# One core, attention and two MLPs: the first table load goes ahead of ScalarE's transfers, the fillers read another tile, and the norm's work moves to the end of the first MLP's steps

## The chip, the core and the metric

The kernel runs on one core of one Trainium2 chip. The time is device microseconds (us) of one launch. The engines are named as in the profile: PE (TensorE, matmuls; PEld is its weight load), ACT (ScalarE), DVE (VectorE), POOL (GpSimd), SP (SyncE, which here only issues transfers). An entry such as ACTq or SPq is an instruction of that engine's queue that the engine itself does not execute, here the issue of a transfer.

## What is computed

Three stages follow each other on 1536 tokens (2 sequences of 768) of width 512, all in float32.

```python
scores = scale * np.matmul(q, k.transpose(0, 1, 3, 2))      # 8 heads of 64
scores = np.where(keep, scores + bias, -1e9)                # keep: first 8 keys, or 96 back
x = softmax(scores) @ v                                     # -> 1536 x 512
h = x @ w_in                                                # 512 -> 2048
x = (h * np.tanh(softplus(h))) @ w_out                      # Mish, 2048 -> 512
xn = x / np.sqrt(np.mean(x * x, -1) + 1e-6) * rms_g
out = (silu(xn @ w_gate) * (xn @ w_val)) @ w_out2           # 512 -> 1536 -> 512
```

The weights arrive as 64-bit words. The kernel turns each piece of them, on the chip, into a high and a low part in a 32-bit format that PE multiplies; a product is then three matmuls (high by high, high by low, low by high).

## The kernel before, in words

**Attention.** There are 48 units: 2 sequences, 4 pairs of heads, 6 tiles of 128 queries. A tile looks at 128 or 256 keys. `scores` (L635) multiplies on PE into two of four PSUM banks, so a unit's scores wait until `soft` has read those of two units before. Behind each unit's scores stands one small matmul as a filler (L649), and in the first four rounds `WARM` larger ones as well (L271, called at L768); the fillers' results are read by nobody. `soft` (L654) adds the bias on DVE (L662) and takes exp on ACT (L672); `norm` (L683) divides on POOL; `transp`, `evac` and `pv` do the product with v. `make_bias` (L620) halves the bias of one head into that of the next on DVE. The bias tile itself is started by four ACT instructions (L743) from maps that DVE makes (L319 to L328). The eight first weight pieces are converted during attention by a fixed plan; the first step of a piece is an ACT instruction on the loaded words (L152).

**The order.** Nothing is scheduled for the author: each engine runs its instructions in the order in which the code emits them. At the start SP and ACT both issue the transfers for the first pair of heads: SP q and k (L245 to L247), ACT v, in two halves of four transfers each (`tiles_v`, L224). ACT's first table load and its first activation (L259) stand behind all eight. The fillers at the very start (L274) read a tile of ones that DVE writes (L261); the fillers in attention read the bias tile (`fill`, L618).

A transfer's completion is counted on one of eight counters that are used in turn, so an issue can wait for the landing of the transfer that last used its counter.

**The first MLP** has 32 steps. A step takes two of the 16 hidden chunks for one block of 384 tokens (four blocks): `products` puts 24 matmuls (L360) in two banks; `mish1` (L495) turns them into g by a chain of tanh, a table load, arctan, sin (ACT, L380 to L386), a multiplication (DVE, L389), a high part (ACT, L486) and a low part (DVE, L490); 18 matmuls (L412) of the step before, in `flush`, stand on PE between this step's products and the next step's. `begin` puts the five bit operations of a next weight piece on DVE (2.7 us for a piece) at the end of the step, two pieces in every eighth step. Steps 24 to 31 hold the last chunks: after step 25's 18 matmuls block 0 is complete, after step 27's block 1, and so on.

**The norm** (`rms_norm`, L451) of a complete block is a list of deferred pieces: squares with row sums on ACT (L457), a power on POOL (L461, L464), the scaling on DVE (L468), and four transposing splits (`split_y`, L436: three PE transposes into bank `s3` at L440, a high part on ACT at L444, a low part on DVE at L445). The squares write their unused result into the same bank `s3`.

```python
        for i in range(2):
            mish.tanh(i)
        do_deferred()
        flush(0)
        do_deferred()
        mish.cosine()
```

`do_deferred` takes one piece from the list. In the first MLP it is called on both sides of `flush`, ahead of the chain's table load. **The second MLP** (`mlp2`, L538, 48 steps of 24 products and 9 accumulating matmuls) calls it in the same two places, and takes what is left of the list.

Of the kernel before, what the change touches and what calls it, by code (L numbers as in the profile page):

```python
# [10 lines left out]
BF16 = mybir.dt.bfloat16  # L11
# [6 lines left out]
P = 128  # L18
# [4 lines left out]
NK = DM // P  # L23
# [3 lines left out]
TB = BT // P  # L27
NBLK = B * S // BT
WPIECE = 512
BANK = 512  # L30
# [8 lines left out]
SLOTS = (10, 14)  # L39

NW_EARLY = 8
WARM = 2

AHEAD = {-4: (0, 2), -3: (2, 4), -2: (4, 6), -1: (6, 8), 0: (8, 12), 1: (12, 16)}

# [5 lines left out]
def tile_attention_mish_swiglu(  # L51
# [16 lines left out]
    pe, act, dve, pool, sp = nc.tensor, nc.scalar, nc.vector, nc.gpsimd, nc.sync  # L68
# [18 lines left out]
    def bank(tag, bufs=1):  # L87
        return psum.tile([P, BANK], F32, tag=tag, bufs=bufs, name=nm(tag))

    def mm_bank():  # L90
        return bank("mm", 4)
# [125 lines left out]
    room = [xypool.tile([P, TB * DM], F32, tag="xy", name=nm("x")) for _ in range(NBLK)]  # L217
# [6 lines left out]
    def tiles_v(v_t, b, p, own=slice(0, NT), queue=None):  # L224


        queue = queue or sp
        vp = v[b][:, p * P : (p + 1) * P]
        vr = vp.rearrange("(t r) e -> r t e", r=P)
        queue.dma_start(v_t[:, own, :], vr[:, own, :])  # L230
        n, last = max(own.start - 1, 0), own.stop - 1
        win = slice(NT + n, NT + last)
        for r in (slice(GLOBAL_MAX, 64), slice(64, P)):
            queue.dma_start(v_t[r, win, :], vr[r, n:last, :])
        queue.dma_start(
            v_t[0:GLOBAL_MAX, win, :],
            vp[0:GLOBAL_MAX].rearrange("r (o e) -> r o e", o=1).to_broadcast(
                (GLOBAL_MAX, last - n, P)
            ),
        )  # L240

    for m in range(2):
        tok = slice(m * BT, (m + 1) * BT)
        own, win = slice(m * TB, (m + 1) * TB), slice(NT + (m and 2), NT + 2 + 3 * m)
        sp.dma_start(q_first[:, tok], qT[0, 0][:, tok])  # L245
        sp.dma_start(k_first[:, own, :], kT[0, 0][:, own, :])
        sp.dma_start(k_first[:, win, :], kT[0, 0][:, win, :])  # L247
        tiles_v(v_first, 0, 0, own, act)

    small = cpool.tile([P, 28], F32, tag="small", name="small")  # L250
    half, mhalf = small[:, 0:1], small[:, 1 : 1 + TB]
# [5 lines left out]
    dve.memset(mhalf, -0.5)  # L257
    dve.memset(half_pi, HALF_PI)
    act.activation(primed, half, AF.Exp)  # L259
    first = room[1][:, 10 * P : 12 * P].bitcast(BF16)  # L260
    dve.memset(first, 1.0)  # L261
    dve.memset(least[:, 0:1], 1.0)
    dve.memset(least[:, 1:4], 0.0)
    dve.memset(most, 0.0)
# [4 lines left out]
    def warm(ps, n, x):  # L269
        for _ in range(n):  # L270
            pe.matmul(ps, x[:, 0:P], x, start=True, stop=True)  # L271

    for _ in range(4):
        warm(mm_bank(), 3, first)  # L274
    ident = cpool.tile([P, P], F32, tag="ident", name="ident")
    make_identity(nc, ident)

# [117 lines left out]
    def begin(n):  # L395
        for _ in range(n):
            begun.append(Piece(started[0]))
            begun[-1]("b3")
            started[0] += 1
# [30 lines left out]
    deferred = []  # L430

    def do_deferred():
        if deferred:
            deferred.pop(0)()

    def split_y(y, blk, kc):  # L436
        t = hl.tile([P, 2, BT], F32R, tag="hl", name=nm("hl"))
        tr = bank("s3")
        for m in range(TB):
            pe.transpose(  # L440
                tr[:, m * P : (m + 1) * P], y[:, m, kc * P : (kc + 1) * P], ident
            )
        g = gcol[:, kc : kc + 1]
        act.activation(t[:, 0, :], tr[:, 0:BT], AF.Copy, scale=g)  # L444
        dve.scalar_tensor_tensor(  # L445
            t[:, 1, :], tr[:, 0:BT], g, t[:, 0, :].bitcast(F32),
            op0=ALU.mult, op1=ALU.subtract,
        )
        ys.setdefault(blk, []).append(t)

    def rms_norm(blk):  # L451
        y = sums[blk]
        ss = cpool.tile([P, 2, TB], F32, tag="ss", name=nm("ss"), bufs=2)

        def square(m):
            junk = bank("s3")
            act.activation(junk, y[:, m, :], AF.Square, accum_out=ss[:, 0, m : m + 1])  # L457

        def inverse():
            square(TB - 1)  # L460
            pool.tensor_scalar(  # L461
                ss[:, 1, :], ss[:, 0, :], 1.0 / DM, 1.0e-6, op0=ALU.mult, op1=ALU.add
            )
            pool.tensor_tensor(ss[:, 0, :], ss[:, 1, :], mhalf, op=ALU.pow)  # L464

        def scale():
            for m in range(TB):
                dve.tensor_scalar(  # L468
                    y[:, m, :], y[:, m, :], ss[:, 0, m : m + 1], None, op0=ALU.mult
                )  # L470

        deferred.append(lambda: [square(m) for m in range(TB - 1)])
        deferred.append(inverse)
        deferred.append(scale)
        deferred.extend([lambda kc=kc: split_y(y, blk, kc) for kc in range(NK)])

    pend = []

# [16 lines left out]
    def mish1(s, mish):  # L495

        blk, cs = s // 2 % NBLK, chunks(s)
        for i in range(2):
            mish.tanh(i)
        do_deferred()  # L500
        flush(0)
        do_deferred()
        mish.cosine()
        old = begun[:]
        del begun[:]
        for piece in old[:1]:
            piece("hi")
        for i in range(2):
            mish.times(i)
        for piece in old[:1]:  # L510
            piece("lo")
        gt = [split_hi(mish.t[:, i, :]) for i in range(2)]
        for piece in old[1:]:
            piece("hi")
        for i in range(2):
            split_lo(gt[i], mish.t[:, i, :])
        for piece in old[1:]:
            piece("lo")
        begin(BEGUN1[s])

        def later():
            def done(m):
                if m == TB - 1 and cs[1] == NC1 - 1:
                    rms_norm(blk)

            for c, g in zip(cs, gt):
                accumulate("out", g, c, blk, done)

        pend.append(later)
# [57 lines left out]
    def attention_banded():  # L587
        fresh()
        mm = [mm_bank() for _ in range(4)]
        with ExitStack() as st:  # L590
# [24 lines left out]
            biases = bp.tile([P, H, 3 * P], BF16, tag="bias", name="bias")  # L615
            bias, bias0 = biases[:, :, 0 : 2 * P], biases[:, :, 2 * P :]

            fill = biases.rearrange("p h k -> p (h k)")[:, 0:BANK]  # L618

            def make_bias(h):  # L620

                dve.tensor_scalar(  # L622
# [7 lines left out]
            first = []  # L630
# [4 lines left out]
            def scores(u):  # L635
                b, p, t = u
                n = width(t) // P
                banks = mm[2:4] if units.index(u) % 2 else mm[0:2]
                for j in range(2):
                    r = slice(64 * j, 64 * j + 64)  # L640
                    pe.matmul(  # L641
                        banks[j][:, 0 : n * P],
                        qs[b, p][r, t * P : (t + 1) * P],
                        ks[b, p][r, 0, :] if t == 0 else ks[b, p][r, t : t + NT : NT - 1, :],
                        start=True,
                        stop=True,
                    )

                pe.matmul(  # L649
                    banks[1][:, 3 * P :], fill[:, 0:P], fill[:, 0:P], start=True, stop=True  # L650
                )
                sc[u] = banks

# [105 lines left out]
            for i in range(-4, nu + 2):  # L759

                def tick(slot, i=i):
                    for k, op in plan.get((i, slot), ()):
                        pieces[k](op)

                if i + 4 < nu:
                    scores(units[i + 4])
                if i < 0:
                    warm(bank("s3"), WARM, fill)  # L768
                if 0 <= i < nu:
                    transp(units[i])  # L770
                if i >= 2:
                    pv(units[i - 2])
                for j in range(*AHEAD.get(i - nu, (0, 0))):
                    c, kc = divmod(j, NK)
                    if kc == 0:
                        first.append(mm_bank())
                    products(first[c], "in", c, xs[0], (kc,))
                if i == nu - 2:
                    mish_first = Mish(first)
                if nu - 2 <= i < nu:  # L780
                    mish_first.tanh(i - nu + 2)
                if 1 <= i <= nu:
                    evac(units[i - 1])
                if 0 <= i + 3 < nu:
                    soft(units[i + 3], tick)
                if 0 <= i + 2 < nu:
                    norm(units[i + 2], tick)
                if -3 <= i < 3:
                    make_bias(i + 5)
                if i >= 2:  # L790
                    evac_out(units[i - 2])
                if i % NT == 2 and 0 <= i // NT:
                    for load, n in ((load_qk, 2), (load_v, 1)):
                        if i // NT + n < B * NPAIR:
                            load(*divmod(i // NT + n, NPAIR))
                tick(3)
                if i == nu - 1:
                    for piece in pieces:
                        piece.rest()
                if i == nu:  # L800
                    mish1(0, mish_first)
# [155 lines left out]
```

## Time and profile before

| | |
|---|---|
| median of 3 runs | 695.7 us (694.32 to 696.01) |
| the profiled execution, its own time | 695.73 us |
| its span from first to last instruction | 693.9 us |
| PE, PEld busy | 673.5 us (97%), 585.2 us (84%) |
| DVE, ACT, POOL busy | 450.2 us (65%), 386.1 us (56%), 68.8 us (10%) |
| granted TensorE clock, mean | 0.993 |
| moved by DMA | 54.20 MB, 78 GB/s over the span |

The busy share of PE is that of a pipelined engine whose ends are modelled. The profiled execution is the source of all durations below; 1.8 us of its own time lie outside of its span. A line of the timeline gives the start in us, how long it lasted in us, the engine, the line of the code, the operation, what is written and read, and how many like instructions are merged in it; in brackets stands how long the engine had been idle before it, and what ended that.

### The profile page before, as it was taken

To read this page: it belongs to the slowest core of one execution; us is meant where nothing else is said; L and a number is where in the kernel's file an instruction comes from. 1 tells how busy PE (TensorE), PEld (TensorE's weight loads), DVE (VectorE), ACT (ScalarE), POOL (GpSimd) and SP (SyncE) were. 2 spreads that over 40 slices of the span, in tenths; PEclk is the share of its full clock that TensorE was granted. 3 is DMA by queue.
4 is the path that set the end of the run, shared out by engine and by line. 5 is a ranking of instruction groups with operands and counts; after the bars stand their busy time and mean duration, and the time that the engine had idled before them with its cause. 6 is when DMAs were issued, how large, how long until landed. Compare 5 with 4: busy or idle time off the path is not lost.

```text
span 693.9 us, 10039 instructions
## 1 busy us (share of the span) xinstructions
PE 673.5 (97%) x3764; PEld 585.2 (84%) x3764; DVE 450.2 (65%) x1067; ACT 386.1 (56%) x722; POOL 68.8 (10%) x128
## 2 busy tenths in 40 slices
PE   7999999999999999999889999999999999999997
PEld 2666668999999999999678889999999999999996
DVE  4878764887788778875866788884268774331232
ACT  3989887888888888887788524322122222111111
POOL 1676770000000000000000001000000000000000
PEclk8999999999999999999999999999999999999999
DMA  8767630122123212211111122230022200010111
GB/s 261 233 209 236 176 104 31 62 91 61 63 68 91 84 60 71 82 61 61 64 58 61 32 79 74 74 109 31 1 61 91 77 16 1 0 46 1 46 47 50
DMA packets 26729, 54.20 MB, mean 78 GB/s; under 512 B 2609, under 2 KB 14641, under 8 KB 26673
## 3 DMA queue, kind: packets, MB, share of 16 engines
q1 hardware_dynamic: 25136, 52.77, 23.9%
q10 hardware_dynamic: 1536, 0.72, 0.4%
q8 instruction: 31, 0.51, 0.3%
q14 instruction: 26, 0.20, 0.1%
HBM read 50.34 MB, written 3.15 MB: 77 GB/s over the span
## 4 chain that ended last, share of the span: by engine, by line
PE 80%; DVE 9%; ACT 9%; issue 1%; DMA 1%; SPq 0%; ACTq 0%
PE mm L360 42%; PE s L412 29%; PE mm L641 3%; PE s L726 2%; ACT e L672 2%; PE s L706 2%; ACT L384 1%; DVE bits L175 1%; DVE e L662 1%; DVE bits L169 1%; ACT d L385 1%; ACT d L386 1%; DVE w L194 1%; DVE g L490 1%; DVE d L389 1%
## 5 line engine op out<-in xcount | busy, mean ns | idle before, releaser
L360 PE MATMUL mm<-hl,w 128*128 128x384 f32 x1920 | 349.6, 336 | 0.0
L360 PEld LDWEIGHTS mm<-hl,w 128*128 128x128 f32 x1920 | 336.2, 188 | 6.9 <-issue 1.0
L412 PE MATMUL s<-w,g 128*128 128x512 f32 x1008 | 246.9, 393 | 4.3 <-ACT g L486 3.0
L412 PEld LDWEIGHTS s<-w,g 128*128 128x128 f32 x1008 | 187.0, 188 | 43.5 <-ACT g L486 4.5
L553 ACT ACTIVATE r<-mm 128x384 f32<-128x384 f32 x48 | 23.5, 490 | 135.3 <-PE mm L360 135.2
L554 DVE TENSOR_TENSOR r<-r,mm 128x384 f32<-128x384 f32 x48 | 26.4, 550 | 68.7 <-ACT r L553 68.7
L424 DVE TENSOR_TENSOR x<-x,s 128x512 f32<-128x512 f32 x60 | 40.2, 686 | 40.2 <-PE s L412 40.2
L486 ACT ACTIVATE g<-r 128x384 fp32r<-128x384 f32 x48 | 25.2, 525 | 69.9 <-DVE r L554 69.9
L389 DVE TENSOR_TENSOR d<-d,mm 128x384 f32<-128x384 f32 x64 | 32.5, 550 | 46.1 <-ACT d L386 46.1
L672 ACT ACTIVATE e<-e,s 128x256 f32<-128x256 f32 (+1 forms) x96 | 46.2, 482 | 11.5 <-DVE s L662 11.1
L691 POOL TENSOR_SCALAR e<-e,s 128x256 f32<-128x256 f32 (+1 forms) x96 | 47.8, 513 | 38.9 <-DVE bias L622 15.1
L169 DVE SCALAR_TENSOR_TENSOR bits<-stage,bits 128x512 int32<-128x512 int32 x68 | 48.2, 708 | 2.1
L175 DVE SCALAR_TENSOR_TENSOR bits<-stage,bits 128x512 int32<-128x512 int32 x68 | 47.2, 694 | 2.0
L490 DVE TENSOR_TENSOR g<-r,g 128x384 fp32r<-128x384 f32 x48 | 26.8, 559 | 28.4 <-ACT g L486 28.4
L486 ACT ACTIVATE g<-d 128x384 fp32r<-128x384 f32 x64 | 33.4, 526 | 16.4 <-DVE d L389 14.5
L384 ACT ACT_TABLE_LOAD x32 | 41.1, 1283 | 0.6
L194 DVE TENSOR_TENSOR w<-bits,w 128x512 fp32r<-128x512 f32 x60 | 41.3, 688 | 0.0
L380 ACT ACTIVATE d<-mm 128x384 f32<-128x384 f32 x64 | 30.4, 492 | 17.5 <-PE mm L360 15.8
L380 ACT ACT_TABLE_LOAD x31 | 39.8, 1283 | 0.5
L662 DVE CUSTOM_DVE_ANT_0 e<-mm,bias 128x256 f32<-128x256 f32 (+1 forms) x96 | 35.2, 396 | 5.1 <-PE mm L641 3.2
L190 ACT ACTIVATE w<-bits 128x512 fp32r<-128x512 f32 x60 | 36.9, 616 | 0.0
L641 PE MATMUL mm<-k,q 64*128 64x256 f32 (+1 forms) x168 | 31.9, 410 | 2.6 <-DVE s L662 2.6
(83 smaller groups left out, 509.7 us busy)
## 6 DMA issues: line engine op xcount, KB each, us to landing
stage<-in_w_out_dram SPq DMA_DIRECT2D x28, 512.0 KB, 3.2
stage<-in_w_in_dram SPq DMA_DIRECT2D x16, 512.0 KB, 4.3
stage<-in_w_gate_dram SPq DMA_DIRECT2D x12, 512.0 KB, 3.5
stage<-in_w_val_dram SPq DMA_DIRECT2D x12, 512.0 KB, 3.4
k<-in_kT_dram SPq DMA_DIRECT2D x7, 704.0 KB, 4.1
out_dram<-x SPq DMA_DIRECT2D x12, 256.0 KB, 2.1
q<-in_qT_dram SPq DMA_DIRECT2D x7, 384.0 KB, 4.7
v<-in_v_dram SPq DMA_DIRECT2D x7, 384.0 KB, 6.1
```

The costliest lines, as they stand in the source:

```text
L169: dve.scalar_tensor_tensor(self.bits, self.lw, 29, self.bits, op0=ALU.logical_shift_right, op1=ALU.bitwise_or,)
L175: dve.scalar_tensor_tensor(self.bits, self.hw, -1073741824, self.bits, op0=ALU.bitwise_and, op1=ALU.bitwise_or,)
L194: engine.tensor_tensor(self.wt[:, 1, :], self.fl, self.wt[:, 0, :].bitcast(F32), op=ALU.subtract)
L360: pe.matmul(ps[:, 0:BT], w[:, wi, col], xs[kc][:, xi, :], start=kc == 0 and i == 0, stop=kc == NK - 1 and i == 2,)
L380: act.activation(self.t[:, i, :], self.h[i], AF.Tanh, scale=0.5)
L384: act.preload_act_table_set("trig_and_small")
L412: pe.matmul(acc[m], gt[:, gi, tok], w[:, wi, :], start=c % 4 == 0 and i == 0, stop=c % 4 == 3 and i == 2,)
L486: act.activation(gt[:, 0, :], x, AF.Copy)
L641: pe.matmul(banks[j][:, 0 : n * P], qs[b, p][r, t * P : (t + 1) * P], ks[b, p][r, 0, :] if t == 0 else ks[b, p][r, t : t + NT : NT - 1, :] ...
L662: dve.tensor_tensor_reduce(e[:, j, 0:n], banks[j][:, 0:n], bias0[:, h, :] if t == 0 else bias[:, h, :], scale=-0.125, scalar=3.0e38, op0=A ...
L672: act.activation(e[:, j, 0:n], e[:, j, 0:n], AF.Exp, scale=-1.0, bias=s[:, 0, j : j + 1], accum_out=s[:, 1, j : j + 1],)
L691: pool.tensor_scalar(e[:, j, 0:n], e[:, j, 0:n], s[:, 3, j : j + 1], 0.0, op0=ALU.mult, op1=ALU.add,)
```

## The change

Three things are changed. At the start, ACT's first activation, and with it the table load, comes ahead of ACT's transfers; of those only the first half of v stays on ACT, and the second half is issued by SP behind q and k. The fillers in attention read the tile of ones instead of the bias tile, and the first four rounds have one large filler instead of two. In the norm, all three squares and the power are one piece, the scaling and the first split are one piece, and the first MLP takes one piece a step, at the end of the step just ahead of `begin`, instead of two pieces around `flush`. The second MLP still takes two.

```diff
-WARM = 2
+WARM = 1
@@ the transfers for the first pair of heads
         sp.dma_start(q_first[:, tok], qT[0, 0][:, tok])
         sp.dma_start(k_first[:, own, :], kT[0, 0][:, own, :])
         sp.dma_start(k_first[:, win, :], kT[0, 0][:, win, :])
-        tiles_v(v_first, 0, 0, own, act)
+        if m:
+            tiles_v(v_first, 0, 0, own)
@@
     act.activation(primed, half, AF.Exp)
-    first = room[1][:, 10 * P : 12 * P].bitcast(BF16)
-    dve.memset(first, 1.0)
+    tiles_v(v_first, 0, 0, slice(0, TB), act)
+    ones = room[1][:, 10 * P : 12 * P].bitcast(BF16)
+    dve.memset(ones, 1.0)
@@ rms_norm
         def inverse():
-            square(TB - 1)
+            for m in range(TB):
+                square(m)
             pool.tensor_scalar(
                 ss[:, 1, :], ss[:, 0, :], 1.0 / DM, 1.0e-6, op0=ALU.mult, op1=ALU.add
             )
@@
-        deferred.append(lambda: [square(m) for m in range(TB - 1)])
         deferred.append(inverse)
-        deferred.append(scale)
-        deferred.extend([lambda kc=kc: split_y(y, blk, kc) for kc in range(NK)])
+        deferred.append(lambda: [scale(), split_y(y, blk, 0)])
+        deferred.extend([lambda kc=kc: split_y(y, blk, kc) for kc in range(1, NK)])
@@ mish1
         for i in range(2):
             mish.tanh(i)
-        do_deferred()
         flush(0)
-        do_deferred()
         mish.cosine()
@@
         for piece in old[1:]:
             piece("lo")
+        do_deferred()
         begin(BEGUN1[s])
@@ attention_banded
-            fill = biases.rearrange("p h k -> p (h k)")[:, 0:BANK]
-
@@ scores
-                    banks[1][:, 3 * P :], fill[:, 0:P], fill[:, 0:P], start=True, stop=True
+                    banks[1][:, 3 * P :], ones[:, 0:P], ones[:, 0:P], start=True, stop=True
@@ the rounds
                 if i < 0:
-                    warm(bank("s3"), WARM, fill)
+                    warm(bank("s3"), WARM, ones)
```

How the order moves is seen in three places. Lines of the changed code are up to two higher or one lower than those of before.

ACT at the start of the program, before (`x` is the room that holds v, `small` the tile of constants):

```order
L230 DMA x_84<-in_v_dram 128x3x128
L234 DMA x_84<-in_v_dram 32x2x128
L234 DMA x_84<-in_v_dram 64x2x128
L235 DMA x_84<-in_v_dram 32x2x128
L230 DMA x_84<-in_v_dram 128x3x128
L234 DMA x_84<-in_v_dram 32x3x128
L234 DMA x_84<-in_v_dram 64x3x128
L235 DMA x_84<-in_v_dram 32x3x128
L259 ACT_TABLE_LOAD
L259 ACTIVATE small<-small 128x1
L299 TENSOR_LOAD flag_i
L743 ACTIVATE bias<-x_85 128x128 x2
```

and now:

```order
L260 ACT_TABLE_LOAD
L260 ACTIVATE small<-small 128x1
L230 DMA x_84<-in_v_dram 128x3x128
L234 DMA x_84<-in_v_dram 32x2x128
L234 DMA x_84<-in_v_dram 64x2x128
L235 DMA x_84<-in_v_dram 32x2x128
L301 TENSOR_LOAD flag_i
L742 ACTIVATE bias<-x_85 128x128 x2
```

The load and the first activation went from behind eight issues to ahead of four; the other four stand on SP between its last L247 and its own load of the flag.

DVE in step 27 of the first MLP, before (`x_84` is block 0's sum, `d` and `g` are this step's):

```order
L175 SCALAR_TENSOR_TENSOR bits_3507<-stage_3292,bits_3507 128x512
L468 TENSOR_SCALAR x_84<-x_84,ss_3488 128x512 x3
L389 TENSOR_TENSOR d_3541<-d_3541,mm_3515 128x384
L389 TENSOR_TENSOR d_3541<-d_3541,mm_3516 128x384
L194 TENSOR_TENSOR w_3575<-bits_3507,w_3575 128x512
L490 TENSOR_TENSOR g_3580<-d_3541,g_3580 128x384
L490 TENSOR_TENSOR g_3582<-d_3541,g_3582 128x384
L154 TENSOR_SCALAR bits_3586<-stage_3364 128x512
```

and now:

```order
L175 SCALAR_TENSOR_TENSOR bits_3507<-stage_3288,bits_3507 128x512
L391 TENSOR_TENSOR d_3541<-d_3541,mm_3515 128x384
L391 TENSOR_TENSOR d_3541<-d_3541,mm_3516 128x384
L194 TENSOR_TENSOR w_3568<-bits_3507,w_3568 128x512
L492 TENSOR_TENSOR g_3573<-d_3541,g_3573 128x384
L492 TENSOR_TENSOR g_3575<-d_3541,g_3575 128x384
L471 TENSOR_SCALAR x_84<-x_84,ss_3484 128x512 x3
L447 SCALAR_TENSOR_TENSOR hl_3582<-s_567_3583,small,hl_3582 128x384
L154 TENSOR_SCALAR bits_3589<-stage_3360 128x512
```

The scaling of block 0 went from ahead of the step's multiplications to behind its low parts, and the first split's low part stands right behind it.

PE between steps 27 and 28, before (`mm_3602` and `mm_3603` are step 28's products, `s_560` to `s_562` the accumulators):

```order
L412 MATMUL s_562_3550<-w_3056,g_3503 128x512 x3
L360 MATMUL mm_3602<-hl_182,w_2688 128x384 x3
...
L360 MATMUL mm_3603<-hl_185,w_2904 128x384 x3
L440 MATMUL s_574_3632<-ident,x_84 128x128 x3
L412 MATMUL s_560_3548<-w_3065,g_3580 128x512 x3
```

and now:

```order
L414 MATMUL s_562_3546<-w_3052,g_3495 128x512 x3
L442 MATMUL s_567_3583<-ident,x_84 128x128 x3
L362 MATMUL mm_3605<-hl_182,w_2684 128x384 x3
...
L362 MATMUL mm_3606<-hl_185,w_2900 128x384 x3
L414 MATMUL s_560_3544<-w_3061,g_3573 128x512 x3
```

The first split's transposes of block 0 stand ahead of step 28's products now, where they stood behind them.

## Rows read from the trace of the kernel before

**Rows 1.** The page, part 1: busy time, share of the span, instructions.

```profile
PE 673.5 (97%) x3764; PEld 585.2 (84%) x3764; DVE 450.2 (65%) x1067; ACT 386.1 (56%) x722; POOL 68.8 (10%) x128
```

**Rows 2.** Timeline of the first 21 us.

```profile
7.38 0.29 DVE L325 TENSOR_TENSOR x<-x 128x128 f32<-128x128 f32 x1
...
7.73 1.28 ACT L259 ACT_TABLE_LOAD   x1 [7.73 <-DMA x<-in_v_dram]
...
9.13 1.10 ACT L743 ACTIVATE bias<-x 128x128 bf16<-128x128 f32 x4
...
9.98 0.29 PE L649 MATMUL mm<-bias 128*128 128x128 bf16 x1 [3.27 <-ACT bias L743]
...
10.33 0.80 SPq L119 DMA_DIRECT2D stage<-in_w_in_dram  x2
...
11.23 1.22 PE L641 MATMUL mm<-x,x 64*128 64x256 f32 x4
...
12.49 0.42 DVE L662 CUSTOM_DVE_ANT_0 e<-mm,bias 128x256 f32<-128x256 f32 x1 [1.59 <-PE mm L641]
...
13.46 1.23 PE L641 MATMUL mm<-x,x 64*128 64x256 f32 x4
13.46 0.24 DVE L622 TENSOR_SCALAR bias<-bias 128x384 bf16<-128x384 bf16 x1
...
19.84 0.50 ACT L672 ACTIVATE e<-e,s 128x256 f32<-128x256 f32 x1
...
20.34 0.66 ACT L152 ACTIVATE bits<-stage 128x512 f32<-128x512 f32 x1
```

**Rows 3.** Waits of SP's queue, 0 to 40 us: total, times, longest.

```profile
SPq L119 <- DMA x<-in_v_dram: 0.7, 1, 0.7
```

**Rows 4.** Issues at 5.3 and 10.3 us: KB each, us to landing.

```profile
x<-in_kT_dram SPq DMA_DIRECT2D x2, 192.0 KB, 4.6
stage<-in_w_in_dram SPq DMA_DIRECT2D x1, 512.0 KB, 5.4
```

**Rows 5.** Half microseconds: busy PE, PEld, DVE, ACT, POOL, granted clock, DMA share, GB/s.

```profile
9.00:9.50 0.50, 0.00 (x0) 0.00 (x0) 0.00 (x0) 0.49 (x4) 0.00 (x0) 0.53 0.39 92
...
15.50:16.00 0.50, 0.50 (x3) 0.32 (x4) 0.39 (x3) 0.50 (x3) 0.06 (x1) 0.64 1.13 424
```

**Rows 6.** Timeline, first MLP: step 26 begins at 317.59, step 25's end.

```profile
317.59 4.35 PE L360 MATMUL mm<-hl,w 128*128 128x384 f32 x24
...
318.95 1.02 DVE L490 TENSOR_TENSOR g<-d,g 128x384 fp32r<-128x384 f32 x2
...
321.78 4.28 PE L412 MATMUL s<-w,g 128*128 128x512 f32 x18
```

**Rows 7.** Timeline, steps 27 to 31 and the second MLP's first.

```profile
325.90 4.35 PE L360 MATMUL mm<-hl,w 128*128 128x384 f32 x24
...
334.98 1.21 POOL L464 TENSOR_TENSOR ss<-ss,small 128x3 f32<-128x3 f32 x1
...
340.26 0.49 PE L440 MATMUL s<-ident,x 128*128 128x128 f32 x3
...
340.51 4.37 PE L412 MATMUL s<-w,g 128*128 128x512 f32 x18
...
376.07 1.27 DVE L468 TENSOR_SCALAR x<-x,ss 128x512 f32<-128x512 f32 x3
...
377.48 4.41 PE L360 MATMUL mm<-hl,w 128*128 128x384 f32 x24
```

**Rows 8.** Timeline, second MLP, steps 4 to 9.

```profile
413.94 0.61 DVE L445 SCALAR_TENSOR_TENSOR hl<-s,small,hl 128x384 fp32r<-128x384 f32 x1
...
418.32 0.58 ACT L457 ACTIVATE s<-x 128x512 f32<-128x512 f32 x1
...
426.75 1.27 DVE L468 TENSOR_SCALAR x<-x,ss 128x512 f32<-128x512 f32 x3
...
442.22 4.35 PE L360 MATMUL mm<-hl,w 128*128 128x384 f32 x24
```

More of the change, by code (lines that the diff above doesn't have):

```diff
@@ L273, in tile_attention_mish_swiglu @@
     for _ in range(4):
-        warm(mm_bank(), 3, first)
+        warm(mm_bank(), 3, ones)
     ident = cpool.tile([P, P], F32, tag="ident", name="ident")
```

## The prediction, made before the changed kernel ran

> **What bounds the kernel.** I read the page's busy shares first, then the timeline of the first 21 us, then the two MLPs step by step. PE is busy 97% of the span [rows 1], so the time is PE's work plus the places where PE has nothing to do or runs slowly. The reader is to see two such places. The first is the start. ACT loads its first table only after eight issues (at 7.73) [rows 2], so the bias tile begins at 9.13, and PE, whose filler reads that tile, idles for 3.27 us up to 9.98. In that idle time the granted clock falls to 0.5, at about 9.0, and it is back only at about 15.9 [rows 5]; meanwhile a unit takes PE 2.23 us (11.23 to 13.46), and DVE waits for it. The second place is the norm. A plain step of the first MLP is 4.18 us of products and 4.12 us of accumulation, 8.30 together (317.59, 321.78, 325.90) [rows 6, 7]. From 325.90, the products of step 27, to 442.22, the products of the second MLP's step 9, pass 116.3 us [rows 7, 8]. Five steps at 8.30, the second MLP's first, which has the same matmuls, at 8.30, eight more at 6.25 (4.18 and half an accumulation) and 16 splits at 0.25 (340.26 to 340.51) [rows 7] are 103.8. So the norm costs PE 12.5 us of waiting today.
>
> **Part 1, the start.** Today ACT's eight issues are over at 7.73; the four that stay, begun a moment later, are over before 7.67, where DVE ends the first map (L325) [rows 2]. That map, no longer the transfers, then releases the bias tile. It starts at 7.7 instead of 9.13. PE's fillers wait for nothing, and the second scores are ready before DVE wants them. The four L743 take 1.1 as now, so the first exp comes at 9.0. From there a unit costs DVE 1.2 us (12.49 to the end of L622 at 13.70), which then sets the pace; PE with one filler less needs about 1.8 us in the slow clock and half of that in the fast one. Unit 5's exp, now at 19.84, would come at about 15.0.
>
> What is late next is the first weight piece. ACT's L152 on it stands right behind that exp, now at 20.34. The piece is issued at 10.33 and lands 5.4 us later, at 15.7 [rows 2, 4]. So the start can give 4.3 us, if the landing slips by no more than 0.3. Does it slip? SP now issues four more transfers ahead of it. SP's issue of the weights is not short of time: it waits 0.7 us for the landing of an earlier transfer, whose counter it uses [rows 3]. In the new order that is the second L247, issued at about 5.4 and landing 4.6 later [rows 4], so at 10.0: the issue stays near 10.35. The next pair's k and q stand just ahead of it, near 9.7; at 4 to 5 us to landing [rows 4] they are there by 15, when unit 6's scores want them. At worst the four issues cost SP their full 2 us, and the landing slips to 17.7: then the start gives 2.5. At best the pace of DVE alone decides, and it gives 4.9. I take **4.3**, nearer to the rows that show SP waiting.
>
> The Trainium skill says otherwise. In "Trainium Kernel Development and Optimization", Key Constraints, transfers issued from several queues share the same 16 engines, and issuing from several at once saves only the sequencer's issue time. By that, giving up ACT's queue costs SP just that issue time, the worst case above, and the sum would be 1.8 us higher; that SP waits there for a landing and not for its turn [rows 3] speaks against it, and a rival below carries it.
>
> The second half of v, issued by SP up to about 8 and landing by 13, is wanted by the fourth unit's product, which by the pace above comes no earlier than 16: nothing. The order of the memset and the renamed tile cost nothing by themselves.
>
> **Part 2, the norm's work.** The 12.5 us go: neither squares nor splits stand in the chain from tanh to the low part any more, and that chain fits. From the end of a step's products to its last low part it takes 6.5 us (313.47, which is 4.12 ahead of 317.59, to 319.97) [rows 6], against 8.3 that PE works meanwhile.
>
> But new waits come. The scaling stands behind the low parts on DVE, and the first split's transposes stand ahead of the next products on PE, so PE must wait for the whole chain of the step whose products it has just made.
>
> - *Step 27, block 0.* Products end at 330.08 as today; accumulation now runs on without a wait to 334.20. The three squares at the end of step 26 push this step's tanh back: 3 x 0.75 us, of which ACT's slack hides 0.3. Low parts end 6.5 + 1.9 later, at 338.5; scaling and transposes take 1.4 (376.07 to 377.48) [rows 7], to 339.9. Without the wait the transposes would be over at 334.45: **5.5**.
> - *Second MLP, step 0, block 1.* The squares start 1 us ahead of the last low part of step 31, at 5.5 us after its products; squares 2.25, POOL 1.4 [rows 7], scaling and transposes 1.4: 10.6. PE's own work there takes 8.4: **2.2**.
> - *Step 2, block 2.* Squares, power and scaling stay, but the transposes no longer come a step later. Between 0 and 1.4, the length of scaling and transposes; near the upper end, since DVE reaches the scaling only behind a weight piece, about when PE is through: **1.3**.
> - *Step 5, block 3.* The squares write bank `s3` and wait for the split's low part (L445, 413.94 + 0.61). They stand ahead of step 4's Silu on ACT, and from the squares to the scaling pass 8.4 us today (418.32 to 426.75) [rows 8], since a multiplication, a low part and a whole weight piece lie between on DVE. So the scaling starts at about 422.5, and the transposes end at 424. Step 5's products begin about when that low part does and are over 4.2 later, with the transposes it would be 418.4: **5.6**.
> - Twice, in steps 3 and 6, two splits still meet in one bank, as today; an estimate of the rest of the 12.5: **1.1**.
>
> Together 15.7 us come for 12.5 that go: **+3.2**. Splits 1 to 3 of block 0 cost nothing, since their input is scaled and the bank is free a step later. All these sums are good to 1 us or so.
>
> **The clock in the new waits.** Two of them leave PE idle for 4 to 5 us with three transposes behind. The row that is nearest is the start: idle since 6.71, PE lost its clock at about 9.0, after 2.3 us [rows 2, 5]. So both long waits should bring 0.5. The price: at the start PE worked 5.9 us in the slow clock (9.98 to 15.9), half of which, 2.9, is the upper end; the lower is 0. I take 2.2 for each, nearer to the upper end because dense products follow the wait at once: **+4.4**.
>
> The Trainium skill's "TensorE: Matmul & The Clock Gate", HAM oscillation, counts the penalty as half of the throttled time. For a stretch as long as that of rows 5 that is 3.4 a fall, and the sum would be 2.4 us higher; but that stretch began 1 us before PE had work, which costs nothing.
>
> **Sum.** The profiled execution took 695.73, as the median of the runs does: 695.7 - 4.3 + 3.2 + 4.4 = **699.0**.
>
> **The rivals.**
>
> 1. *The clock holds.* Mechanism and place as above; it decides whether a 5 us wait, in which three transposes run, is enough. For it: only the start shows a fall. Against: that fall came after half as long a wait. 695.7 - 4.3 + 3.2 = **694.6**, not slower. Chance 0.14.
> 2. *One of the two waits keeps the clock*, because its transposes fall well: **696.8**. Chance 0.13.
> 3. *A third fall*, at the second MLP's step 0, where PE waits 2.2 us with slow transposes: as long as the start's idle time up to the fall. **701.2**. Chance 0.14.
> 4. *The first weights land 2 us later*, by SP's four issues, and hold ACT at L152: the start gives 2.5. **700.8**. Chance 0.11.
>
> That the change doesn't do what it says (a filler that still waits for the bias) has no ground in the order and hardly a chance.
>
> **How the numbers follow.** The forecast, both long waits slow and 4.3 at the start, has 0.48, and its own range is 697.3 to 700.7. About 0.3%, 2.1 us, is what a measurement of this kernel can tell from no change. Slower by that is above 697.8: most of the forecast, rivals 3 and 4, a third of rival 2: 0.66. Faster is below 693.6: rival 1 with a start of 4.9 and shorter waits: 0.08. The rest, 0.26, is the same. The range goes from rival 1 with its slack to rival 3 with its own: 694.8 to 702.3.
>
> **What would show it.** Right: L742 at about 7.7; exps about 1.25 us apart from 9.0; L152 at about 16; attention over 4 us earlier; steps 28 to 31 without a wait; PE idle for about 5 us before the first transposes in step 27 and in the second MLP's step 5, with a clock of 0.5 behind each. Wrong: L152 near 18 (rival 4); a clock of 1.0 after the waits (rival 1); or transposes that start without waiting for the scaling.

## The result, and the profile after

The change makes the kernel slower: 702.31 us, the median of six runs (700.74 to 704.0), against 695.81 for the kernel before in the same session. The ratio is 1.0101, with a 95% interval of 1.009 to 1.0113, so about 6.5 us more where 3.3 were forecast. The profiled execution took 700.8 us (span 699.0, mean granted clock 0.989); it is the second fastest of the six, which matters below.

PE is as busy as it was in [rows 1], over a span that is 5.1 us longer:

```profile
PE 674.5 (96%) x3760; PEld 589.4 (84%) x3760; DVE 451.1 (65%) x1067; ACT 386.8 (55%) x722; POOL 70.2 (10%) x128
```

**The start** did as foreseen at first. The timeline of the changed kernel (columns as in [rows 2]):

```profile
7.76 1.15 ACT L742 ACTIVATE bias<-x 128x128 bf16<-128x128 f32 x4 [5.55 <-DVE x L327]
...
9.85 0.42 SPq L604 DMA_DIRECT2D q<-in_qT_dram  x1
10.31 1.07 SPq L119 DMA_DIRECT2D stage<-in_w_in_dram  x2
...
12.91 0.60 PE L705 MATMUL s<-ident,e 128*128 128x128 f32 x4
...
15.41 0.49 PE L640 MATMUL mm<-k,q 64*128 64x128 f32 x4 [1.89 <-DVE s L688]
...
16.63 0.66 ACT L152 ACTIVATE bits<-stage 128x512 f32<-128x512 f32 x1 [1.38 <-DMA stage<-in_w_in_dram]
```

The bias begins at 7.76 instead of 9.13, and L152 at 16.63 instead of 20.34. But between 13.5 and 15.4 PE has nothing to do: its next matmul is unit 6's scores, and they need the second pair's q. (The releaser in brackets is only inferred here; in a later profile it is that transfer.) The list of issues gives the landings, to be set against [rows 4]: KB each, us to landing.

```profile
stage<-in_w_in_dram SPq DMA_DIRECT2D x1, 512.0 KB, 6.3
q<-in_qT_dram SPq DMA_DIRECT2D x1, 384.0 KB, 5.4
```

The q issued at 9.85 landed at about 15.3, and the first weights, issued at 10.31, at about 16.6. In all, step 27 of the first MLP begins at 322.06 instead of 325.90 [rows 7]: the start gave 3.8 us in this execution.

**The norm.** The waits of PE from 320 to 450 us (total, times, longest):

```profile
PE s L442 <- DVE x L471: 11.8, 4, 4.6
PE s L442 <- DVE hl L447: 0.5, 2, 0.3
```

The same view of the kernel before has no wait for the scaling (L468) among its waits:

```profile
PE s L412 <- ACT g L486: 3.0, 4, 1.1
PE s L440 <- DVE hl L445: 2.4, 4, 1.6
PE s L412 <- DVE g L490: 1.2, 5, 0.2
```

The timeline of the changed kernel from step 27 to the second MLP's step 9, which answers to [rows 7, 8]:

```profile
322.06 4.35 PE L362 MATMUL mm<-hl,w 128*128 128x384 f32 x24
...
326.24 4.28 PE L414 MATMUL s<-w,g 128*128 128x512 f32 x18
...
333.59 1.02 DVE L492 TENSOR_TENSOR g<-d,g 128x384 fp32r<-128x384 f32 x2
334.52 1.27 DVE L471 TENSOR_SCALAR x<-x,ss 128x512 f32<-128x512 f32 x3
335.15 1.18 PE L442 MATMUL s<-ident,x 128*128 128x128 f32 x3 [4.63 <-DVE x L471]
335.98 5.57 PE L362 MATMUL mm<-hl,w 128*128 128x384 f32 x24
...
377.90 1.03 PE L442 MATMUL s<-ident,x 128*128 128x128 f32 x3 [2.13 <-DVE x L471]
378.69 5.98 PE L414 MATMUL s<-w,g 128*128 128x512 f32 x18
...
422.42 1.18 PE L442 MATMUL s<-ident,x 128*128 128x128 f32 x3 [4.38 <-DVE x L471]
423.25 4.16 PE L414 MATMUL s<-w,g 128*128 128x512 f32 x9
...
447.47 4.35 PE L362 MATMUL mm<-hl,w 128*128 128x384 f32 x24
```

The reader is to see four waits for the scaling where the kernel before had none: in step 27, and in the second MLP's steps 0, 2 (0.69 us) and 5. The matmuls behind three of them are longer than usual (5.57 us for 24 products, 5.98 for 18 and 4.16 for nine accumulating matmuls, where 4.35, 4.28 and 2.24 are plain). Windows of 1 us (columns as in [rows 5]) show why:

```profile
335.00:336.00 1.00, 0.85 (x4) 0.51 (x4) 0.80 (x3) 0.00 (x0) 0.00 (x0) 0.54 0.00 0
...
380.00:381.00 1.00, 1.00 (x4) 0.81 (x3) 0.20 (x1) 0.00 (x0) 0.00 (x0) 0.50 0.00 0
...
421.00:422.00 1.00, 0.00 (x0) 0.00 (x0) 0.97 (x3) 0.00 (x0) 0.00 (x0) 0.50 0.00 0
```

The clock falls to 0.5, the lower of its two levels (1.2 GHz instead of 2.4), three times, for 3.4, 3.4 and 6.8 us. From step 27's products to those of the second MLP's step 9 pass 447.47 - 322.06 = 125.4 us, where it was 116.3. By the working of the prediction (103.8 us without any loss) that is 21.6 us of waits and slow work, instead of 12.5.

### The profile page after: what moved, and what is told of

Its sections match the earlier page's. It is cut to its first block, busy times and chain, and to the rows that moved or that the text cites. A ratio compares the mean times of both kernels' runs of the same rounds, so it can differ in the third digit from the quotient of the medians.

```text
span 699.0 us, 10036 instructions
## 1 busy us (share of the span) xinstructions
PE 674.5 (96%) x3760; PEld 589.4 (84%) x3760; DVE 451.1 (65%) x1067; ACT 386.8 (55%) x722; POOL 70.2 (10%) x128
## 4 chain that ended last, share of the span: by engine, by line
PE 81%; DVE 8%; ACT 8%; issue 1%; POOL 1%; DMA 0%; DVEq 0%; SPq 0%; ACTq 0%; POOLq 0%
PE mm L362 43%; PE s L414 31%; PE mm L640 2%; PE s L725 2%; ACT e L671 2%; PE s L705 1%; DVE e L661 1%; ACT s L459 1%; DVE x L426 1%; PE s L442 1%; ACT g L488 1%; DVE hl L447 1%; DVE hl L353 1%; DVE bits L175 1%; ACT hl L352 1%
## 5 line engine op out<-in xcount | busy, mean ns | idle before, releaser
L414 PEld LDWEIGHTS s<-w,g 128*128 128x128 f32 x1008 | 190.2, 190 | 36.8
L690 POOL TENSOR_SCALAR e<-e,s 128x256 f32<-128x256 f32 (+1 forms) x96 | 47.9, 513 | 35.0 <-DVE bias L621 10.2
## 6 DMA issues: line engine op xcount, KB each, us to landing
k<-in_kT_dram SPq DMA_DIRECT2D x7, 704.0 KB, 4.2
```

What stands on the lines that cost most here:

```text
L414: pe.matmul(acc[m], gt[:, gi, tok], w[:, wi, :], start=c % 4 == 0 and i == 0, stop=c % 4 == 3 and i == 2,)
L690: pool.tensor_scalar(e[:, j, 0:n], e[:, j, 0:n], s[:, 3, j : j + 1], 0.0, op0=ALU.mult, op1=ALU.add,)
```

## Experiments

Each is compared with runs of the kernel before on the same chip in the same session. Inside the start part only the place of the late half of v and the filling of one wait were varied: how its gain divides between the earlier table load, the fillers' other tile and the one filler less was not tested.

### The two parts apart

`e1_start` is the kernel before with the hunks of the start alone, `e2_norm` with those of the norm alone.

> The kernel before with the start part of the change alone (table load ahead of ACT's transfers, half of v on SP, fillers on the tile of ones, one large filler). Theory: the parts add up, and the start gives what the trace of the change shows at the products of step 27, 317.59 + 8.31 - 322.06 = 3.8 us, so 692.0, with L152 at about 16.6 and no slow clock before it. Rival: part of those 3.8 us is lost again in the attention's end or the first MLP of this order, then 693 to 695.

> The kernel before with the norm part alone. Theory: the median of the change plus the 3.8 us of the start, 706.1, with three stretches of clock 0.5 (step 27's end, the second MLP's steps 0 and 5). Rival: the falls depend on how the program lies against the clock's own rhythm, and without the start part one of them stays out or is shorter: 703 to 704.

Measured: the start alone 694.45 (before 695.65; ratio 0.9976, 0.9963 to 0.9989), the norm alone 703.87 (1.012, 1.0104 to 1.0137). So -1.2 and +8.2, together 7.0, where the change as a whole gave 6.5: the parts add up, but the start gives far less than the 3.8 us of the changed kernel's trace. Both rivals came nearer than the theory, the first one only in its number: in the profile of `e1_start` 368.2 us pass from step 27 to the end, against 368.0 in that of the kernel before, so what is missing was lost ahead of step 27. The 12 runs of the start alone reach from 691.52 to 695.23. In the profile of `e2_norm` the clock falls twice in the norm, not three times, as its rival had it. That of `e1_start` shows what differs from the trace above, in its windows:

```profile
15.50:16.00 0.50, 0.50 (x8) 0.41 (x4) 0.23 (x3) 0.00 (x0) 0.50 (x2) 0.77 1.05 336
16.00:17.00 1.00, 1.00 (x7) 0.53 (x6) 0.28 (x4) 0.28 (x1) 0.38 (x1) 0.50 1.02 357
```

The same windows of the changed kernel:

```profile
15.50:16.00 0.50, 0.50 (x6) 0.38 (x7) 0.00 (x0) 0.00 (x0) 0.50 (x2) 1.00 1.16 336
16.00:17.00 1.00, 1.00 (x11) 0.66 (x11) 0.51 (x4) 0.37 (x1) 0.41 (x1) 1.00 0.95 304
```

In `e1_start` the clock falls behind the wait for q, and step 27 begins 1.44 us later than in the changed kernel's profile (323.50 against 322.06). The same fall is in the profiles of `e3_filled`, `e4_apart` and `e5_spread` below; of the five profiles with the new start and nothing else done at that wait, the changed kernel's own is the only one without it. So the profiled execution is a lucky one, and the median of 702.31 lies 1.5 us above it.

### Filling the waits

`e3_filled` is the changed kernel with work for PE in the waits for the scaling; `e6_fill_q` is the start alone with work in the wait for q; `e11_both_filled` is the changed kernel with both.

```diff
+    def busy(blk):
+        x = xs[NBLK - 1][0] if blk == 0 else ys[0][0]
+        junk = bank("s3")
+        for _ in range((20, 9, 2, 20)[blk]):
+            pe.matmul(junk[:, 0:BT], x[:, 0, 0:P], x[:, 0, :], start=True, stop=True)
...
-        deferred.append(lambda: [scale(), split_y(y, blk, 0)])
+        deferred.append(lambda: [scale(), busy(blk), split_y(y, blk, 0)])
```

And ahead of unit 6's scores:

```diff
+                if i == 2:
+                    warm(bank("s3"), 7, ones)
                 if i + 4 < nu:
                     scores(units[i + 4])
```

> The changed kernel with extra matmuls on PE (20, 9, 2 and 20 of 128x384, some 0.18 us each, result unused) ahead of the first split's transposes of blocks 0 to 3, so that PE works through most of each wait for the scaling. Theory, waits and clock apart: the waits stay (the transposes start at the same time after the step's products), the clock keeps 1.0, and the three slow stretches with their 1.6, 2.3 and 2.2 us go: about 695.5. Rival: the waits are the whole loss and the slow stretches cost next to nothing: 701 to 702. Second rival: the clock falls all the same, since something else than the wait brings it down: 702.

> The start part alone, with seven matmuls of 128x512 on the tile of ones ahead of unit 6's scores, where PE waits about 2 us for the second pair's q. Theory, the clock: the fall at about 15.5 stays out in every run and the start gives its 3.8 us in all of them: 692.0, and the runs lie within 1.5 us. Rival, the transfers: the runs of the start part differ because the landing of q or of the first weights does, and filling changes nothing: 694.5, spread as before.

> The changed kernel with both fillings, the seven matmuls ahead of unit 6's scores and the 20, 9, 2 and 20 ahead of the first splits, so that no fall of the clock is left in it. Theory, the change's loss is 17.0 for 12.5 us of waits in the norm and falls of the clock: the filled start part (692.3) plus 4.5 = 696.8, the clock 0.5 only at the very end. Rival: a part of the loss is something else, and it stays above 698.

Measured: `e3_filled` 698.0 (before 695.65; 1.0037, 1.0024 to 1.0049), `e6_fill_q` 692.34 (before 695.91; 0.9946, 0.9932 to 0.996; all runs within 691.85 to 692.65), `e11_both_filled` 696.54 (before 695.84; 1.0012, 1.0003 to 1.0021). In the last the clock stays at 1.0 from its start to 694 us, and the transposes wait as before for the scaling, behind the filling; the timeline of step 27:

```profile
330.29 3.66 PE L457 MATMUL s<-hl 128*128 128x384 f32 x20
335.08 1.03 PE L442 MATMUL s<-ident,x 128*128 128x128 f32 x3 [1.14 <-DVE x L477]
335.87 4.41 PE L362 MATMUL mm<-hl,w 128*128 128x384 f32 x24
```

Step 28 begins 13.9 us behind step 27's 321.98, as in the changed kernel (13.92), but its products take 4.41 instead of 5.57. So waits and clock are told apart. With the clock held, the norm's stretch takes 120.8 us in this profile: 17.0 us of waits. The falls in the norm are worth 6.5 - 2.35 = 4.15 us in the medians (`e3_filled` against the change), the one in the start 2.35 - 0.70 = 1.65 here, and 3.6 - 1.2 = 2.4 with the start alone. `e3_filled` missed its expected 695.5 by what its own profile shows: the fall behind the wait for q, which then also had its releaser named.

```profile
15.70 0.80 PE L646 MATMUL mm<-k,q 64*128 64x128 f32 x4 [2.34 <-DMA q<-in_qT_dram]
```

`e6_fill_q` bears out that this fall is what spread the runs: its five lie within 0.8 us, where the 12 of `e1_start` had 3.7.

### What delays q

`e7_v_late` is the start alone, with the second half of v issued later on SP.

```diff
-        if m:
-            tiles_v(v_first, 0, 0, own)
...
             conv_prefetch(2)
+            tiles_v(v_first, 0, 0, slice(TB, NT))
```

> The start part alone, with the second half of v issued on SP behind the second pair's k and q and the first two weight pieces instead of ahead of them. Theory, SP's issues delay q: q goes out about 1 us earlier and lands by 14.3, PE waits under 1 us for unit 6, the clock holds there; 691 to 692.5. Rival, the landing is set by the bytes in flight and not by the turn on SP: q still lands after 15, the clock still falls: 694 to 695. Second rival: the late half of v becomes the next wait, PE at the fourth unit's product: 695 or more.

Measured: 690.65 (before 695.91; 0.9927, 0.9913 to 0.9941). Timeline of `e7_v_late`:

```profile
7.27 0.42 SPq L603 DMA_DIRECT2D q<-in_qT_dram  x1
...
14.20 0.49 PE L640 MATMUL mm<-k,q 64*128 64x128 f32 x4 [0.83 <-DMA q<-in_qT_dram]
...
15.46 0.68 ACT L152 ACTIVATE bits<-stage 128x512 f32<-128x512 f32 x1 [0.36 <-DMA stage<-in_w_in_dram]
```

PE waits 0.83 us instead of 1.89, the clock holds, and L152 comes at 15.46. The theory holds in its result. But q went out 2.6 us earlier than in the changed kernel (7.27 against 9.85) and was there only 1.2 earlier: the rival has its share, since from 13 to 16 us the 16 DMA engines are full in either kernel (a share of 0.85 to 1.16 in half microseconds). The second rival is out: nothing waits for the late half of v.

### The norm in other orders

`e4_apart` is the changed kernel with the scaling and the first split as two pieces:

```diff
-        deferred.append(lambda: [scale(), split_y(y, blk, 0)])
-        deferred.extend([lambda kc=kc: split_y(y, blk, kc) for kc in range(1, NK)])
+        deferred.append(scale)
+        deferred.extend([lambda kc=kc: split_y(y, blk, kc) for kc in range(NK)])
```

> The changed kernel with the scaling and the first split as two pieces again, all else as changed. Theory: the transposes no longer wait for a scaling of the same piece in the first MLP, so the wait of step 27 goes and the clock holds there; in the second MLP both pieces of a step still follow each other on both sides of the accumulation. Some 9 of the 21.6 us of waits and slow stretches stay or fewer: 686 to 690. Rival: the place at the end of the step is what costs, whatever stands in one piece: 698 or more.

Measured: 688.91 (before 695.65; 0.9896, 0.9877 to 0.9914). So it is not the place at the end of the step that costs, but the scaling and the transposes that need it in one piece. The waits of PE from 312 to 450 us in `e4_apart`:

```profile
PE s L442 <- DVE hl L447: 2.9, 4, 1.0
PE s L414 <- ACT g L488: 0.8, 1, 0.8
PE s L414 <- DVE g L492: 0.2, 1, 0.2
```

From step 27 to the second MLP's step 9 it takes 110.5 us, 6.7 over the 103.8. What is left is mostly the second of two splits in a step, which waits for its bank.

`e5_spread` puts squares, weight piece and scaling in one step and then one split a step, in both MLPs; `e8_spread_fill` is that with the filled wait for q.

```diff
+    def do_norm():
+        if norms:
+            norms.pop(0)()
...
         do_deferred()
+        do_norm()
         begin(BEGUN1[s])
+        do_norm()
```

> The changed kernel with the norm spread out: squares and power at the end of the step in which the block is complete, the scaling behind that step's weight piece, and from the next step on one split a step, in both MLPs. Theory, the norm's loss is PE waiting for the scaling and for the bank of a second split in the same step: nearly all of the 17.0 us of waits that the filled kernel shows goes, 1 to 3 us stay, and no clock falls there: 681 to 685. Rival: DVE, which gets the scaling on top of a weight piece in one step, becomes late for the next chain and PE waits there instead: 688 or more.

> The kernel with the spread norm, and the seven matmuls ahead of unit 6's scores. Theory: the start and the norm are independent, so it lies below the kernel with the spread norm by what the filled start lies below the start part alone, some 2 us: 680 to 683. Rival: what the start gains is lost again at another wait: the same as the kernel with the spread norm.

Measured: `e5_spread` 689.36 (before 695.91; 0.9897, 0.9883 to 0.9911), `e8_spread_fill` 687.27 (0.988, 0.9865 to 0.9896). The difference of 2.1 us is about what the filled start is worth (2.4 above), so start and norm are independent. But both lie some 4 us above the range expected. The rival has the size, yet not the engine: at the largest wait of `e5_spread` it is ACT that comes late. The timeline of `e5_spread`, from step 28's end to step 29's matmuls:

```profile
348.03 0.61 ACT L464 ACTIVATE s<-x 128x512 f32<-128x512 f32 x1 [1.10 <-DVE hl L452]
...
351.58 0.87 ACT L382 ACTIVATE d<-mm 128x384 f32<-128x384 f32 x2
...
356.87 0.74 PE L414 MATMUL s<-w,g 128*128 128x512 f32 x2 [1.83 <-ACT g L495]
```

The squares write their unused result to bank `s3`, which the split's low part still reads. ACT waits 1.10 us for that, then squares for 2.2, and the tanh behind them is late by the sum. Behind the wait of 1.83 us the clock falls as well (0.5 from 357.5 to 360.9). A second wait, of 1.49 us in `e5_spread` and 2.33 in `e8_spread_fill`, has another cause: in the second MLP's step 0 the next split's transposes want bank `s3`, while the low part of the split before (L452) still stands behind step 31's chain on DVE. The timeline of `e8_spread_fill`:

```profile
374.93 0.55 PE L447 MATMUL s<-ident,x 128*128 128x128 f32 x3 [2.33 <-DVE hl L452]
```

### A version ahead of both

`e9_apart_v_late` joins `e4_apart` and `e7_v_late`. `e10_planned_v_late` gives every piece its step instead, with the same later v; `e12_planned_own_junk` is `e10_planned_v_late` with a tile of their own for the squares.

```diff
+    first_split = (28, 32, 36, 40)
+    first_norm = (26, 29, 31, 33)
+    def do_split(s):
+        for blk in range(NBLK):
+            if 0 <= s - first_split[blk] < NK:
+                work[blk][2 + s - first_split[blk]]()
+    def do_norm(s):
+        for blk in range(NBLK):
+            if 0 <= s - first_norm[blk] < 2:
+                work[blk][s - first_norm[blk]]()
```

The tile of its own:

```diff
+    junk = cpool.tile([P, DM], F32, tag="junk", name="junk")
...
-            junk = bank("s3")
             act.activation(junk, y[:, m, :], AF.Square, accum_out=ss[:, 0, m : m + 1])
```

> The changed kernel with the scaling and the first split apart, and the second half of v issued behind the first two weight pieces. Theory: the gains add, 688.9 less the 3.8 us by which the later v lies below the start part alone: 685.1. Rival: with PE ahead in the start another wait takes part of it: 686.5 or more.

> The same later v, and the norm's pieces at fixed steps: never two splits in one step, squares and power at the end of steps 26, 29, 31 and of the second MLP's step 1, the scaling a step later, ahead of that step's weight piece. Theory: the waits for the bank of a second split (2.9 us in the kernel with the pieces apart) go too, and DVE never has scaling, two low parts of splits and a weight piece together: 2 to 4 us of waits stay, 681 to 684. Rival: the squares in steps 29 and 31 make ACT late for the next chain, and it is no better than the kernel with the pieces apart: 685 or more.

> The kernel with the pieces at fixed steps and the later v, whose squares now write a tile of their own in SBUF instead of bank s3. Theory, the shared bank: in steps 29 and 31 the squares no longer wait for the split's low part (1.1 us each), the second MLP's first split no longer waits for the squares (1.2), and no clock falls behind it: 682 to 683.5. Rival, ACT's time: the squares' own 2.25 us ahead of the next tanh are what makes PE wait, and the time stays within 1 us of 685.6.

Measured: `e9_apart_v_late` 686.21 (before 695.84; 0.9855, 0.9838 to 0.9872), 1.1 us above the sum of the gains. In its profile no wait of the start or the norm takes that: step 27 begins at 321.11 (`e7_v_late` 320.87), and from there to the second MLP's step 9 it takes 110.4 us (`e4_apart` 110.5). What is longer is the end: from PE's last matmul to the end of the span 6.3 us pass, against 5.3 in `e4_apart`, since the last transfer of the result lands later. Whether that holds in its other runs is not shown. `e10_planned_v_late` 685.62 (0.9855, 0.9835 to 0.9875), so the rival: no splits meet, but the second MLP's first split waits for the squares, and the clock falls there. The timeline of `e10_planned_v_late`:

```profile
371.72 0.60 ACT L466 ACTIVATE s<-x 128x512 f32<-128x512 f32 x1 [1.07 <-DVE hl L454]
...
374.01 0.55 PE L449 MATMUL s<-ident,x 128*128 128x128 f32 x3 [1.19 <-ACT s L466]
374.31 5.94 PE L412 MATMUL s<-w,g 128*128 128x512 f32 x18
```

`e12_planned_own_junk` 682.69 (before 694.78; 0.9824, 0.981 to 0.9837), 12 us below the kernel before: it was the shared bank. Against its own runs of before it gains 12.1 us where `e10_planned_v_late` gained 10.2, so the bank is worth 1.9 us by that measure and 2.9 by the two medians. In its profile these lines read:

```profile
368.40 0.62 ACT L467 ACTIVATE junk<-x 128x512 f32<-128x512 f32 x1
...
370.52 0.49 PE L449 MATMUL s<-ident,x 128*128 128x128 f32 x3
370.76 4.37 PE L412 MATMUL s<-w,g 128*128 128x512 f32 x18
```

## Why the prediction was wrong in size

The sign and the mechanism were right, the size was not: +3.3 forecast, +6.5 measured, and 702.31 lies a hair above the range. Term by term, with the medians of the runs (each against its own runs of before):

| term | forecast | measured | from |
|---|---|---|---|
| start, clock held | -4.3 | -3.6 | `e6_fill_q` |
| clock in the start | 0 | +1.65 | `e3_filled` less `e11_both_filled` |
| norm's waits, clock held | +3.2 | +4.3 | `e11_both_filled` less `e6_fill_q` |
| clock in the norm | +4.4 | +4.15 | the change less `e3_filled` |
| sum | +3.3 | +6.5 | |

The four measured terms are differences between neighbouring kernels, so that they add up is no test of them; what bears them out are the profiles (3.5 us from the filled start at step 27, 17.0 for 12.5 us of waits, 4.6 for the clock in the norm).

**The step that failed** is the sentence on the next pair's k and q: that they are there by 15, "when unit 6's scores want them". They were there at about 15.3, but PE wanted them at 13.5. Unit 6's scores are next on PE as soon as unit 5's are through, while unit 5's exp comes only at 14.66, and the prediction had worked out the exps alone. The cost put at nothing was a wait of 1.7 to 2.4 us on PE, and behind it, in four of five profiles, a fall of the clock like the one that the change had just taken away at 9 us. This is the largest single miss, 1.65 us.

**The start's own size** (0.7 us short). The issue of the first weights stayed at 10.31, with 10.35 forecast, but not for the reason given, so this number held by luck. The counter that they use was to be free at 10.0, 4.6 us after the second L247; that transfer was there after 2.6, at 8.2:

```profile
5.60 0.33 SPq L247 DMA_DIRECT2D x<-in_kT_dram  x1
```

SP's view of the changed kernel has no wait of L119 for a landing any more. Before, SP lost 2.9 us to four such waits between the second L247 and the weights; now its own four issues, from 5.97 to 8.34, take their place, and where they come later, in `e7_v_late`, the weights go out at 7.73:

```profile
7.73 0.90 SPq L119 DMA_DIRECT2D stage<-in_w_in_dram  x2
```

What slipped was the landing, 6.3 us instead of the 5.4 of [rows 4], where k and q now go out only 0.9 and 0.5 us ahead of it (1.7 and 1.0 before); L152 came at 16.63 and not at 16. Rival 4 had put 2 us on the landing and was nearer to the mechanism than to the size. The sentence of the Trainium skill ("Trainium Kernel Development and Optimization", Key Constraints), that issuing from several queues saves only issue time, would, as an estimate, have given 700.8. The traces agree with it: in `e7_v_late`, without the four issues ahead of them, SP issues the weights 2.6 us earlier, and from 13 to 16 us the same 16 engines are full in either kernel.

**The norm's waits** (1.1 us short). Place by place, from `e11_both_filled`: step 27 5.3 (forecast 5.5), the second MLP's step 0 2.9 (2.2), step 2 1.5 (1.3), step 5 5.2 (5.6), steps 3 and 6 1.3, and 0.8 in pieces of under 0.2 in the other steps, where 1.1 was forecast for these last two together. The replay of the chain was good to 0.7 us everywhere (for step 5 its own rows give 6.0, since 413.94 + 0.61 + 8.4 is 422.95 and not 422.5); the rest is the many small waits that it left out.

**The clock in the norm** came out at the forecast sum by two errors that cancel. There were three falls in the profile of the change, so rival 3's place was right, and two in that of `e2_norm`. But each cost about 1.5 us, not 2.2: from step 27 to the second MLP's step 9 the change took 125.4 us against 120.8 with the clock held, 4.6 for three, and `e2_norm` 123.8, 3.0 for two. By the rule in "TensorE: Matmul & The Clock Gate", HAM oscillation, of the Trainium skill (half of the throttled time) the stretches of 3.4, 3.4 and 6.8 would, as an estimate, have cost 6.8. The measured 4.6 decides: 2.0 us of the third stretch passed while PE had no work (up to 422.42), as in [rows 5], which takes 1.0 off, and why the rest is 1.2 below the rule is open.

Of the signs that the prediction named, L742 at 7.76, steps 28 to 31 without a wait, and the two long waits with 0.5 behind them are as written, and the exps are nearly so (1.1 to 1.5 us apart from 9.6); L152 and the attention's end are 0.6 and 0.5 us late.

## What to carry to other kernels

When a piece of work is joined to the one that feeds it, look at which engine stands in between: a scaling on DVE and transposes of its result on PE in one piece made PE wait for a whole chain, while the same two pieces, called apart, lie some 13 us below that (`e4_apart`). When a start is pulled ahead, ask for every engine at what time it wants its next input and not only for the one that sets the pace, since a wait of 2 us in which PE has nothing to do can cost as much again in the clock behind it. A profile is one execution: before its numbers are taken for the kernel's, compare its time and its mean clock with those of the other runs.

## What had not been expected of the hardware

The same wait keeps the clock in one execution and loses it in another, and its length alone does not tell which: after 1.89 us for q it held in the changed kernel's profile, after 1.69 us in `e1_start` it fell; after the 2.1 us in the second MLP's step 0 it fell in the changed kernel and held in `e2_norm`. The slow stretch behind the wait for q was 3.4 us in the profile of `e1_start` and 6.8 in that of `e3_filled`, where step 27 then began at 323.50 and 325.23 (322.06 without a fall). So the runs of one kernel spread: 3.7 us in the 12 of `e1_start`, 0.8 in the five with the wait filled. Seven matmuls that compute nothing were worth 2.1 us (`e5_spread` to `e8_spread_fill`) to 2.4 (`e1_start` to `e6_fill_q`, each against its own runs of before).
